# Three results written by VectorE behind the last maximum, later banks for output tiles and exponentials in pairs: an attention and feed-forward kernel on one core

## The chip, the cores and the metric

The kernel runs on one core of a Trainium2 chip. The metric is the device time of one execution in microseconds (us), as the median of several runs. The engines of the core are named as in the profile: PE (matrix products; PEld is its weight loading), DVE (VectorE), ACT (ScalarE), POOL (GpSimd) and SP (SyncE, which issues all DMAs here). SBUF is the on-chip memory; PSUM has eight banks of 512 fp32 columns, into which PE writes.

## The reference

The input x has 2048 rows of 512 values. It is normalized by row; an attention block with 32 heads of 16 values and a gated feed-forward block of width 1792 both take the normalized rows, and their results are added to x:

```python
xn = _layernorm(x, axis=-1)
q, k, v = (xn @ wqkv), split into 32 heads of 16
p = softmax(q @ k.T * 16 ** -0.5)          # 2048 x 2048 for each head
attention = (p @ v, heads side by side) @ wo
ffn = (silu(xn @ w1) * (xn @ w3)) @ w2
out = x + attention + ffn
```

## The kernel before, in words

**Tiling.** The query rows are cut into four blocks of 512 (`qc`), the 32 heads into eight groups of four (`g`). One block and group make a piece of work that is cut into units: two of 256 query rows, and for the last four groups four of 128 rows. In the last group of the last block the four units are called A, B, C and D here; D is the last unit of the kernel.

**What a unit goes through.**

- Maxima: PE computes scores with 128 query rows on the partitions (L1041, two banks at a time), and DVE takes the maximum of each row (L1081, 1024 columns at a time). From these come the negated maximum `negm` (L1217 on DVE for the last units, POOL otherwise) and two bf16 values of it, `Z` (L1165, L1167).
- Query tile: for the last four units `Z` is added to the query by a PE tile named `AQ` (`tile_QT2`), whose result ACT writes to `QT` (L810). Earlier units get it by DMA.
- Scores: PE computes them again, now with the keys on the partitions (L1303). One block of four matmuls of 128 columns fills one bank and is the input of one exponential. ACT takes the exponential of a bank (L1316, 512 columns) or of two neighbouring banks in one instruction (L1346, 1024 columns) and writes to a slot of `PT`.
- Value products: PE multiplies `PT` by the values (`tile_PV`, emitted at L566). For the last three units (B, C, D) it also sums the exponentials with a matrix of ones, DVE takes the reciprocal (L1402) and multiplies (L1404). For the units before, A among them, ACT copies the bank to `U` (L1412); then follow a DMA to `Lc` (L1433), a power on POOL (L1437), a DMA to memory (L1442), a DMA back to all partitions (`R`, L1446) and a product on POOL (L1457). The result is the normalized head `ON`.
- Output: rows of the first three blocks are finished by `tile_OUT`. For each 128 rows of the last block, `tile_OUTA` sums x, the feed-forward part and the first six head groups, and ACT writes the sum to one of four buffers (`t1`, `a32`, `th`, `zg`; L938). `tile_OUTB` multiplies the last two head groups by `wo`, DVE adds the buffer (L952), and SP issues the store (L907).

**What sets the order.** Nothing is ordered by the hardware here: a planner in Python (`_Prog` and the `pick_` functions) keeps a model of when each engine is free and when each operand is ready, picks in each step the operation that can start first, and writes the order out, with semaphore waits between engines. PE's candidates are the scores of L1041 (`p1_cand`), those of L1303 (`p2_cand`), the groups of matmuls of the active tiles (`col_cand`) and filling matmuls (`fill_cand`), whose results nobody reads.

**Banks.** Until the last maximum is issued, banks 0 to 3 belong to the maxima and banks 7, 6, 5, 4 to everything else; from then on (`red_n[0] >= NP1`) all eight are shared. A tile is a tenant of its bank from `give` until its result is written. `assign` hands out banks to tiles, `score_bank` chooses a bank for a score block, and `p2_cand` lets at most four blocks wait for their exponential. In the last stretch `assign` starts a new tile while fewer than five banks have tenants, and the `OUTB` tiles, in order, take a bank as soon as their `OUTA` is written; the tile then waits for its heads group by group (`g_on`). `exp_pair` makes one instruction of two blocks when their banks are neighbours and the second is ready within 0.02 us of the planner's model (`PAIR_WAIT`).

**Queues.** A tile's result goes to `miscq` (ACT) or to `redq` (DVE), which is served first in, first out; the items for `Z` of the last unit are put at its head.

**Filling.** `fill_cand` adds matmuls of the identity while a running count of PE columns (`low_load`) is under a bound.

Of the kernel before, what the change touches and what calls it, by code (L numbers as in the profile page):

```python
# [8 lines left out]
ALU = mybir.AluOpType  # L9
# [244 lines left out]
def _build(nc, A_x, A_wqkv, A_wo, B_w1, B_w3, B_w2, out):  # L254
# [19 lines left out]
    PAIR_DEPTH = 3  # L274
    PAIR_GAP = 1
    LAZY_GAP = 0.02
    MIN_PIECE = 1
    HI_LEAD = 0.0
    LAZY_MAX = 3.0
# [3 lines left out]
    MATE = 0.0  # L283
# [64 lines left out]
    with ctx:  # L348
# [449 lines left out]
        def tile_QT2(u):  # L798
            qc, g, q0, nq = units[u]
            qs = (qc * NG + g) % 3  # L800
            par = u % 2
            groups = qt_groups(qc, g, q0, nq, False)
            for qt in range(nq // 128):
                groups.append((lambda bk, qt=qt: col_groups(
                    bk, lambda i, z=32: Z[:, par, qt, 32 * i:32 * i + z], lambda i: ident[:, :], 128, c0=qt * 128,
                    start=False, stop=True, skip=True),
                    [("Z", par), ("ident",)], _c_mm(128), None))

            def evac(bk):
                return [_Item(lambda e: e.activation(QT[:, qs, q0:q0 + nq], bank(bk)[:, 0:nq], ACTF.Identity),  # L810
                              [("ps", bk)], qh_keys(qs, q0, nq), _c_act(nq), cb=lambda op: done.add(("AUG", u)))]
            return _Tile("AQ%d" % u, groups, evac, need=-1, cols=4 * nq)
# [97 lines left out]
        def tile_OUT(tg):  # L910
# [4 lines left out]
            def evac(bk):  # L915
                def cb(op):
                    store(tg)
                    done.add(("OUT", tg))
                    if tg + NXR < NT:
# [5 lines left out]
                         and all(("hT", qc * FC + fc) in done for fc in range(FC))  # L925
                         and all(("ON", qc, g, ts) in done for g in range(NG)), paced=True)

        def tile_OUTA(tg):
            qc, ts = divmod(tg, 4)
            groups = [g_x(tg)] + [g_h(tg, fc, NGA == 0 and fc == FC - 1) for fc in range(FC)]  # L930
            groups += [g_on(qc, ts, g, False, g == NGA - 1) for g in range(NGA)]

            def evac(bk):
                def cb(op):
                    done.add(("OUTA", tg))
                    if tg + NXR < NT:
                        load_xr(tg + NXR)
                return [_Item(lambda e: e.activation(opart[ts], bank(bk), ACTF.Identity),  # L938
                              [("ps", bk)], OP_KEYS[ts], _c_act(512), cb=cb)]
            return _Tile("OUTA%d" % tg, groups, evac, pred=lambda: ("xr", tg) in done  # L940
                         and all(("hT", qc * FC + fc) in done for fc in range(FC))
                         and all(("ON", qc, g, ts) in done for g in range(NGA)))

        def tile_OUTB(tg):
            qc, ts = divmod(tg, 4)
            groups = [g_on(qc, ts, g, g == NGA, g == NG - 1) for g in range(NGA, NG)]

            def evac(bk):
                def cb(op):
                    store(tg)  # L950
                    done.add(("OUT", tg))
                return [_Item(lambda e: e.tensor_tensor(osb[:, tg % 4, :], bank(bk), opart[ts], ALU.add),  # L952
                              [("ps", bk)] + OP_KEYS[ts], [("osb", tg % 4)], _c_dve(512), cb=cb)]
            return _Tile("OUTB%d" % tg, groups, evac, pred=lambda: ("OUTA", tg) in done and ("ST", tg - 4) in done)


        def split_rows(u):
# [292 lines left out]
        def score_bank(up=False):  # L1250
            mates = {it.exp[0] for it in expq[-1:]}
            best = (None, 0.0)
            for b in pool_banks():
                if b in bank_tenant or b in p2_busy:
                    continue
                r = P.ready("pe", (), [("ps", b)])
                if b - 1 in mates or (b + 1 in mates and not up):
                    r -= MATE
                if best[0] is None or r < best[1] - 1e-6:
                    best = (b, r)  # L1260
            return best

        def p2_cand():
# [2 lines left out]
                return None  # L1266
            n = p2_n[0]
            b, b_rd = score_bank()
            if b is None or len(p2_busy) >= 4:
                return None  # L1270
            qc, g, q0, nq = units[u]
            kpb = 512 // nq
# [82 lines left out]
        def tile_PV(u):  # L1355
# [37 lines left out]
            def evac(bk):  # L1393
# [15 lines left out]
                def cb(op):  # L1409
                    nrm_wait.append(u)  # L1410
                    nrm_next()
                return [_Item(lambda e: e.activation(U[:, us, 0:nq], bank(bk)[:, 0:nq], ACTF.Identity),  # L1412
                              [("ps", bk)], [("U", us)], _c_act(nq), cb=cb)]
            return _Tile("PV%d" % u, groups, evac, cols=4 * nq)
# [116 lines left out]
        def assign():  # L1531
# [17 lines left out]
            if crit and crit[0].name.startswith("AQ"):  # L1549
                bk = free_bank(TILE_BANKS if p2_n[0] and red_n[0] < NP1 else None)[0]  # L1550
                if bk is not None:
                    give(crit.pop(0), bk)
            if not head_tiles and sum(b in bank_tenant for b in pool_banks()) < (1 if red_n[0] < NP1 else 5):
                bk = free_bank(TILE_BANKS if red_n[0] < NP1 else None)[0]
                t = None if bk is None else choose()
                if t is not None:
# [15 lines left out]
        def col_cand():  # L1572
# [34 lines left out]
            def emit():  # L1607
# [8 lines left out]
                if not t.groups:  # L1616
# [8 lines left out]
                        if cb0 is not None:  # L1625
                            cb0(op)
                    last.cb = cb
                    if t.name.startswith("OUTB") or (t.name.startswith("PV") and int(t.name[2:]) in FAST_PV):
                        redq.extend(items)
                    else:  # L1630
                        miscq.extend(items)
# [141 lines left out]
        def pick_act():  # L1773
            a = cand("act", expq[0]) if expq else None
            pair, mate = None, 0
            for k in range(1, min(len(expq), PAIR_DEPTH)):
# [3 lines left out]
                if two is None:  # L1780
                    continue
                a2 = cand("act", two)
                if a2 <= a + PAIR_WAIT and (red_n[0] >= NP1 or sum(b_ in bank_tenant for b_ in pool_banks()) <= PAIR_TEN):
                    a, pair, mate = a2, two, k
                    break
            m = None
# [155 lines left out]
```

## Time and profile before

| what | before |
|---|---|
| time, median of 3 runs | 1196.95 us (1196.06 to 1197.04) |
| the profiled execution | 1196.41 us, of which the span from first to last instruction is 1194.7 us |
| busy: PE, DVE, ACT, POOL | 97%, 98%, 98%, 38% of the span |
| granted TensorE clock, mean | 0.999 |
| maxima on DVE (L1081) | 1018 instructions, 1217 ns each |
| single exponentials on ACT (L1316) | 1680 instructions, 628 ns each |
| paired exponentials on ACT (L1346) | 184 instructions, 1075 ns each |
| last maximum ends, last exponential ends | about 1170.5 us, 1189.2 us from the span's start |

A row of a timeline gives the start in us from the span's start, the time from there to the end of the last instruction of the group, the engine, the line, the operation, what it writes and reads with the shapes, the count, and in brackets the idle time before with what ended it. Neighbouring instructions of one engine overlap by a few hundredths to some tenths of a us, so lengths add up to more than the time that passes. Matmul records show the length of one pass through the array, which overlaps the next.

### The profile page before, as it was taken

The page shows a single profiled execution, that of the slowest core. Times are in us where ns is not written, and L with a number is a line of the kernel's source. Part 1 is how long each engine was busy: PE and PEld are TensorE (multiplying, and loading weights), DVE is VectorE, ACT ScalarE, POOL GpSimd, SP SyncE. Part 2 cuts the span into 40 slices and gives each one's busy share as a digit, 9 for nine tenths or more (in the row PEclk, how much of TensorE's full clock was granted, in tenths as well). Part 3 has the DMA queues.
Part 4 walks back from the last instruction along what each step waited for, and adds up shares of the span by engine and source line. Part 5 has one row for each costly group of instructions (what it writes and reads, how often), then busy time and mean ns, then how long its engine had stood idle before and what let it go on. Part 6 is the DMA issues. An engine that isn't in the chain of part 4 may idle for free.

```text
span 1194.7 us, 33930 instructions
## 1 busy us (share of the span) xinstructions
PE 1154.4 (97%) x14172; PEld 482.5 (40%) x14172; DVE 1172.0 (98%) x1067; ACT 1169.5 (98%) x2236; POOL 455.3 (38%) x912
## 2 busy tenths in 40 slices
PE   9999999999999999999999999999999999999998
PEld 4433333333334333333334434343333333345554
DVE  8999999999999999999999999999999999999994
ACT  7899999999999999999999999999999999999997
POOL 4453752433432255343422236634222215333320
PEclk9999999999999999999999999999999999999999
DMA  6523222111111021111100122211000111000000
GB/s 183 128 59 83 68 65 79 39 33 41 38 24 36 25 71 40 41 32 31 33 20 24 35 59 51 51 31 37 22 20 20 32 33 43 19 22 18 18 18 25
DMA packets 131189, 52.17 MB, mean 44 GB/s; under 512 B 100068, under 2 KB 131036, under 8 KB 131036
## 3 DMA queue, kind: packets, MB, share of 16 engines
q1 hardware_dynamic: 131036, 50.01, 16.9%
q8 instruction: 111, 1.82, 0.7%
q14 instruction: 42, 0.34, 0.1%
HBM read 38.73 MB, written 6.74 MB: 38 GB/s over the span
## 4 chain that ended last, share of the span: by engine, by line
PE 45%; ACT 44%; DVE 6%; issue 2%; DMA 2%; POOL 1%; ACTq 0%; POOLq 0%
ACT PT L1316 30%; PE ps L562 17%; PE ps L1303 13%; PE ps L566 8%; ACT PT L1346 7%; PE ps L1041 7%; DVE part L1081 6%; ACT zg L856 2%; ACT th L850 1%; ACT ub L860 1%; DMA R<-rd 1%; ACT U L1412 1%; ACT kq L750 1%; PE ps L1663 1%; DMA Lc<-U 0%
## 5 line engine op out<-in xcount | busy, mean ns | idle before, releaser
L1081 DVE TENSOR_REDUCE part<-ps 128x2 f32<-128x1024 f32 x1018 | 1153.0, 1217 | 1.9 <-PE ps L1041 1.7
L1316 ACT ACTIVATE PT<-ps 128x512 bf16<-128x512 f32 x1680 | 889.2, 628 | 5.6 <-PE ps L1303 2.5
L1303 PE MATMUL ps<-QT,KT 32*128 32x256 bf16 (+1 forms) x4672 | 544.5, 259 | 4.7 <-ACT PT L1346 3.7
L1041 PE MATMUL ps<-KT,QT 32*128 32x512 bf16 x2042 | 424.3, 384 | 2.4 <-DVE part L1081 2.3
L1303 PEld LDWEIGHTS ps<-QT,KT 32*128 32x128 bf16 x4672 | 207.4, 92 | 214.1 <-issue 110.7
L1437 POOL TENSOR_TENSOR Rc<-Lc,mone 128x8 f32<-128x8 f32 (+1 forms) x70 | 105.9, 1513 | 294.6 <-DMA Lc<-U 294.4
L1346 ACT ACTIVATE PT<-ps 128x1024 bf16<-128x1024 f32 x184 | 194.6, 1075 | 0.0
L562 PE MATMUL ps<-xnT,ident 128*128 128x512 bf16 (+3 forms) x646 | 177.4, 341 | 17.5 <-DVE part L1081 6.7
L566 PE MATMUL ps<-PT,Vaug 128*17 128x256 bf16 (+1 forms) x4672 | 179.6, 261 | 3.1 <-ACT PT L1316 1.3
L562 PE MATMUL ps<-xnT,w 128*128 128x512 bf16 (+3 forms) x637 | 153.2, 321 | 4.7 <-ACT ub L860 1.3
L1041 PEld LDWEIGHTS ps<-KT,QT 32*128 32x128 bf16 x2042 | 107.8, 91 | 122.5 <-DVE part L1081 56.8
L566 PEld LDWEIGHTS ps<-PT,Vaug 128*17 128x17 bf16 x4672 | 84.2, 89 | 89.1 <-issue 69.5
L562 PEld LDWEIGHTS ps<-xnT,ident 128*128 128x128 bf16 x646 | 47.4, 97 | 99.9 <-ACT PT L1316 44.5
L562 PEld LDWEIGHTS ps<-xnT,w 128*128 128x128 bf16 x637 | 44.9, 97 | 85.6 <-issue 52.9
L562 PE MATMUL ps<-w,hT 128*128 128x512 bf16 (+3 forms) x330 | 75.1, 315 | 0.0
L837 POOL TENSOR_TENSOR a<-zg,ub 128x512 f32<-128x512 bf16 x56 | 64.5, 1152 | 21.6 <-ACT ub L860 21.6
L839 POOL TENSOR_TENSOR hT<-a,t 128x512 bf16<-128x512 f32 x56 | 71.0, 1267 | 2.4
L1188 POOL TENSOR_TENSOR mx<-part 128x16 f32<-128x16 f32 (+1 forms) x67 | 14.1, 210 | 141.0 <-DVE part L1081 140.5
L1457 POOL TENSOR_TENSOR wk_on<-U,R 128x256 bf16<-128x256 f32 (+1 forms) x37 | 23.3, 630 | 85.8 <-DMA R<-rd 85.6
L835 POOL TENSOR_SCALAR t<-th 128x512 f32<-128x512 bf16 x56 | 34.7, 619 | 44.8 <-ACT th L850 43.2
L1457 POOL TENSOR_TENSOR on_b<-U,R 128x256 bf16<-128x256 f32 (+1 forms) x33 | 23.4, 709 | 70.9 <-DMA R<-rd 70.9
L850 ACT ACTIVATE th<-zg 128x512 bf16<-128x512 bf16 x56 | 37.7, 673 | 0.0
(104 smaller groups left out, 574.5 us busy)
## 6 DMA issues: line engine op xcount, KB each, us to landing
w<-in_B_w_dram SPq DMA_DIRECT2D x112, 128.0 KB
R<-rd SPq DMA_DIRECT2D x55, 128.0 KB
QT<-qd SPq DMA_DIRECT2D x31, 128.0 KB
KT<-kd SPq DMA_DIRECT2D x28, 128.0 KB
PT<-in_A_x_dram SPq DMA_DIRECT2D x4, 512.0 KB
xr<-in_A_x_dram SPq DMA_DIRECT2D x16, 128.0 KB
out_dram<-osb SPq DMA_DIRECT2D x16, 128.0 KB
qd<-kq SPq DMA_DIRECT2D x15, 128.0 KB
```

The costliest lines, as they stand in the source:

```text
L562: return e.matmul(bank(bk)[:, c0 + a:c0 + b], make_lhsT(0, 128), rhs_ap(0)[:, a:b], start=start, stop=stop, **kw)
L566: ins = e.matmul(bank(bk)[32 * i:32 * i + m, c0 + a:c0 + b], make_lhsT(i), rhs if (a, b) == (0, ncols) else rhs[:, a:b], start=start, stop ...
L837: q.append(_Item(lambda e: e.tensor_tensor(a32[:, :], zg[:, ss, :], ub[:, ss, :], ALU.mult), [("zg", ss), ("ub", ss)], [("a32",)], 1.1, 1.25))
L839: q.append(_Item(lambda e: e.tensor_tensor(hT[:, hslot(idx), :], a32[:, :], t1[:, :], ALU.mult), [("a32",), ("t1",)], [("hT", hslot(idx))] ...
L850: lazyq.append(_Item(lambda e: e.activation(th[:, ss, :], zg[:, ss, :], ACTF.Tanh), [("zg", ss)], [("th", ss)], 0.52, cb=part_done))
L1041: ins = e.matmul(bank(2 * sl + i), QT[32 * j:32 * j + 32, qs, q * 128:(q + 1) * 128], KT[32 * j:32 * j + 32, g, c_ * 512:(c_ + 1) * 512], ...
L1081: redq.append(_Item(lambda e: e.tensor_reduce(dst, pair_ap.rearrange("p (a b) -> p a b", b=512), AX.X, ALU.max), writes, [("part", par, qt ...
L1303: ins = e.matmul(bank(b)[:, i * nq:(i + 1) * nq], KT[32 * j:32 * j + 32, g, (k0 + i) * 128:(k0 + i + 1) * 128], QT[32 * j:32 * j + 32, qs, ...
L1316: expq.append(_Item(lambda e: e.activation(PT[:, sl, :], bank(b), ACTF.Exp, scale=SCALE), [("ps", b)], [("PT", sl)], _c_act(512), cb=cb, e ...
L1346: return _Item(lambda e: e.activation(PT[:, s0:s1 + 1:s1 - s0, :], ps8[:, b0:b1 + 1:b1 - b0, :], ACTF.Exp, scale=SCALE), [("ps", b0), ("ps ...
L1437: poolq["nrm"].append(_Item(lambda e: e.tensor_tensor(Rc[:, pp, 0:nl], Lc[:, pp, 0:nl], mone[:, 0:nl], ALU.pow), [("Lc", pp), ("mone",)], ...
L1457: poolq["nrm"].append(_Item(lambda e: e.tensor_tensor(onorm[ob][:, g, q0:q0 + nq], U[:, us, 0:nq], R[:, pp, 0:nq], ALU.mult), [("U", us)] ...
```

## The change

It concerns only decisions that the planner makes from the last maximum on; the constants that hold before that point stay as they were.

- `to_dve()` is true once the last score block for the maxima has been put on PE. A tile that finishes then has its result written by DVE with a `tensor_scalar` (times 1, plus 0) instead of by ACT: an `AQ` tile (`QT`), an `OUTA` tile (one of the four buffers), a `PV` tile of a unit without the fast path (`U`). Such an item is named `dve` and goes to `redq`.
- An `OUTB` tile gets a bank only when its last two head groups are finished; the last of them (`OUTB_EARLY`) when all but the last group is.
- A new tile is started while fewer than two banks have tenants (`TAIL_TEN`), not five.
- A bank beside the one of the last waiting score block is preferred even if it is ready up to 0.3 us later (`TAIL_MATE`); before, by 0.0.
- Two blocks are paired if the second is ready within 0.05 us (`TAIL_WAIT`), not 0.02.
- `TAIL_BUSY` is 4, the number that was written there before.

```diff
+    OUTB_EARLY = 1
+    TAIL_BUSY = 4
+    TAIL_TEN = 2
+    TAIL_MATE = 0.3
+    TAIL_WAIT = 0.05
+    TAIL_DVE = 1
...
+        def to_dve():
+            return TAIL_DVE and p1_n[0] >= NP1
+
...
             def evac(bk):
+                if to_dve():
+                    return [_Item(lambda e: e.tensor_scalar(QT[:, qs, q0:q0 + nq], bank(bk)[:, 0:nq], 1.0, 0.0,
+                                                            ALU.mult, ALU.add),
+                                  [("ps", bk)], qh_keys(qs, q0, nq), _c_dve(nq), cb=lambda op: done.add(("AUG", u)),
+                                  name="dve")]
                 return [_Item(lambda e: e.activation(QT[:, qs, q0:q0 + nq], bank(bk)[:, 0:nq], ACTF.Identity),
                               [("ps", bk)], qh_keys(qs, q0, nq), _c_act(nq), cb=lambda op: done.add(("AUG", u)))]
...
+                if to_dve():
+                    return [_Item(lambda e: e.tensor_scalar(opart[ts], bank(bk), 1.0, 0.0, ALU.mult, ALU.add),
+                                  [("ps", bk)], OP_KEYS[ts], _c_dve(512), cb=cb, name="dve")]
                 return [_Item(lambda e: e.activation(opart[ts], bank(bk), ACTF.Identity),
                               [("ps", bk)], OP_KEYS[ts], _c_act(512), cb=cb)]
...
-            return _Tile("OUTB%d" % tg, groups, evac, pred=lambda: ("OUTA", tg) in done and ("ST", tg - 4) in done)
+            return _Tile("OUTB%d" % tg, groups, evac, pred=lambda: ("OUTA", tg) in done and ("ST", tg - 4) in done
+                         and all(("ON", qc, g, ts) in done for g in range(NGA, NG if tg < NT - OUTB_EARLY else NG - 1)))
...
                 if b - 1 in mates or (b + 1 in mates and not up):
-                    r -= MATE
+                    r -= MATE if red_n[0] < NP1 else TAIL_MATE
...
-            if b is None or len(p2_busy) >= 4:
+            if b is None or len(p2_busy) >= (4 if red_n[0] < NP1 else TAIL_BUSY):
                 return None
...
+                if to_dve():
+                    return [_Item(lambda e: e.tensor_scalar(U[:, us, 0:nq], bank(bk)[:, 0:nq], 1.0, 0.0,
+                                                            ALU.mult, ALU.add),
+                                  [("ps", bk)], [("U", us)], _c_dve(nq), cb=cb, name="dve")]
                 return [_Item(lambda e: e.activation(U[:, us, 0:nq], bank(bk)[:, 0:nq], ACTF.Identity),
                               [("ps", bk)], [("U", us)], _c_act(nq), cb=cb)]
...
-            if not head_tiles and sum(b in bank_tenant for b in pool_banks()) < (1 if red_n[0] < NP1 else 5):
+            if not head_tiles and sum(b in bank_tenant for b in pool_banks()) < (1 if red_n[0] < NP1 else TAIL_TEN):
...
-                    if t.name.startswith("OUTB") or (t.name.startswith("PV") and int(t.name[2:]) in FAST_PV):
+                    if items[0].name == "dve" or t.name.startswith("OUTB") or (t.name.startswith("PV") and int(t.name[2:]) in FAST_PV):
                         redq.extend(items)
...
-                if a2 <= a + PAIR_WAIT and (red_n[0] >= NP1 or sum(b_ in bank_tenant for b_ in pool_banks()) <= PAIR_TEN):
+                if a2 <= a + (PAIR_WAIT if red_n[0] < NP1 else TAIL_WAIT) and (red_n[0] >= NP1 or sum(b_ in bank_tenant for b_ in pool_banks()) <= PAIR_TEN):
```

The order that the planner writes out for the changed kernel is the same as before on all engines until the last maximum. Behind it the three `tensor_scalar` writes stand on DVE directly after the two `Z` writes (`zg`, then `U`, then `QT`), and ACT's last stretch reads, with x for a count of single exponentials and P for a pair:

```
before: x11 zg x1 U x1 P QT x9 P x2 P x16
after:  x12 P x2 P x1 P x5 P x1 P x1 P x1 P P x1 P x1 P x1
```

## The prediction

> **What bounds the kernel now.** I read the page's totals first, then the order of instructions built from both kernels, then the timelines of the last 31 us, engine by engine, and last the chain of waits there.
>
> ```profile
> span 1194.7 us, 33930 instructions
> PE 1154.4 (97%) x14172; PEld 482.5 (40%) x14172; DVE 1172.0 (98%) x1067; ACT 1169.5 (98%) x2236; POOL 455.3 (38%) x912
> ```
>
> Three engines are full over the whole span, so totals decide nothing. The built order does: all five engines have the same order in both kernels up to the last score maximum; PE first differs just behind the block of 4 scores at 1169.11, ACT at the twelfth exponential of its last stretch, DVE behind the two Z writes. So only the tail counts, from about 1169.5 us to the end. It lasts 25 us; ACT carries it, and its timeline is:
>
> ```profile
> 1164.11 5.58 ACT L1316 ACTIVATE PT<-ps 128x512 bf16<-128x512 f32 x11
> 1169.57 0.61 ACT L938 ACTIVATE zg<-ps 128x512 f32<-128x512 f32 x1
> 1170.05 0.62 ACT L1316 ACTIVATE PT<-ps 128x512 bf16<-128x512 f32 x1
> 1170.61 0.28 ACT L1412 ACTIVATE U<-ps 128x128 f32<-128x128 f32 x1
> 1170.99 0.60 ACT L1316 ACTIVATE PT<-ps 128x512 bf16<-128x512 f32 x1
> 1171.48 1.02 ACT L1346 ACTIVATE PT<-ps 128x1024 bf16<-128x1024 f32 x1
> 1172.38 0.28 ACT L810 ACTIVATE QT<-ps 128x128 bf16<-128x128 f32 x1
> 1173.08 1.57 ACT L1316 ACTIVATE PT<-ps 128x512 bf16<-128x512 f32 x3 [0.41 <-PE ps L1303]
> 1175.28 3.04 ACT L1316 ACTIVATE PT<-ps 128x512 bf16<-128x512 f32 x6 [0.63 <-PE ps L1303]
> 1178.21 1.03 ACT L1346 ACTIVATE PT<-ps 128x1024 bf16<-128x1024 f32 x1
> 1179.13 1.23 ACT L1316 ACTIVATE PT<-ps 128x512 bf16<-128x512 f32 x2
> 1180.26 1.02 ACT L1346 ACTIVATE PT<-ps 128x1024 bf16<-128x1024 f32 x1
> 1181.16 8.05 ACT L1316 ACTIVATE PT<-ps 128x512 bf16<-128x512 f32 x16
> ```
>
> Columns: start, length, engine, line, what, count, idle before. Neighbours overlap, so I count by pitch, from one start to the next. The last row: 8.05 less one length of 0.62, over 15 steps, is 0.495 for a single exponential. A pair takes 0.90 (1171.48 to 1172.38), 0.92 (1178.21 to 1179.13) and 0.90 (1180.26 to 1181.16); I use 0.91. The last exponential ends at 1189.21.
>
> Ledger from 1169.57 to 1189.09, where a next instruction could start: 29 singles 14.36, 3 pairs 2.73, the zg write 0.48 (to 1170.05), U and QT about 0.16 each (1152.53 to 1152.68 is such a step elsewhere), in all 17.89 of 19.52. So **1.63 us are gaps**. Behind 1175.28, where 24 singles and 2 pairs make 13.70 of 13.81, only 0.11. The gaps sit between 1170 and 1175.3, where PE is late.
>
> ```profile
> 1152.53 0.27 ACT L1412 ACTIVATE U<-ps 128x128 f32<-128x128 f32 x1
> 1152.68 2.56 ACT L1316 ACTIVATE PT<-ps 128x512 bf16<-128x512 f32 x5
> ```
>
> ```profile
> 1169.11 0.39 PE L1303 MATMUL ps<-QT,KT 32*128 32x128 bf16 x4
> 1169.43 1.13 PE L566 MATMUL ps<-PT,Vaug 128*17 128x128 bf16 x68
> 1170.56 0.78 PE L1303 MATMUL ps<-QT,KT 32*128 32x128 bf16 x12
> ...
> 1171.82 0.40 PE L562 MATMUL ps<-xnT,wq_last 128*128 128x128 bf16 x4
> ...
> 1173.53 0.23 PE L566 MATMUL ps<-PT,Vaug 128*17 128x128 bf16 x4
> ...
> 1174.53 0.39 PE L562 MATMUL ps<-wo,wk_on 128*128 128x512 bf16 x1
> 1174.85 0.42 PE L1303 MATMUL ps<-QT,KT 32*128 32x128 bf16 x12
> 1175.20 1.18 PE L562 MATMUL ps<-wo,wk_on 128*128 128x512 bf16 x4
> ...
> 1189.27 0.23 PE L566 MATMUL ps<-PT,Vaug 128*17 128x128 bf16 x4 [0.89 <-ACT PT L1316]
> ...
> 1191.28 0.40 PE L562 MATMUL ps<-wo,wk_on 128*128 128x512 bf16 x1 [1.39 <-DVE wk_on L1404]
> ```
>
> PE runs 72 value products from 1169.43 without a score between them; the next 12 scores (three exponentials) start at 1170.56. Behind ACT's last exponential stands a fixed end: products at 1189.27, then
>
> ```profile
> 1162.48 8.02 DVE L1081 TENSOR_REDUCE part<-ps 128x2 f32<-128x1024 f32 x7
> ...
> 1170.95 0.18 DVE L1167 TENSOR_TENSOR Z<-negm,Z 128x4 bf16<-128x4 f32 x1
> 1174.65 0.96 DVE L1402 RECIPROCAL R<-ps 128x128 f32<-128x128 f32 x1 [3.53 <-PE ps L566]
> 1175.64 0.29 DVE L1404 TENSOR_TENSOR wk_on<-ps,R 128x128 bf16<-128x128 f32 x1
> ...
> 1189.94 0.96 DVE L1402 RECIPROCAL R<-ps 128x128 f32<-128x128 f32 x1 [4.86 <-PE ps L566]
> ...
> 1191.72 0.69 DVE L952 TENSOR_TENSOR osb<-ps,zg 128x512 bf16<-128x512 f32 x1 [0.49 <-PE ps L562]
> ```
>
> the reciprocal, the last output product and the last sum to 1192.41, and 2.29 us for the store. From the end of the last exponential to the span's end that is 5.49 us. The changed order ends with the same instructions, so the time follows the end of ACT's last exponential. DVE, between 1171.13 and 1174.65, stands idle: room for three moved writes.
>
> **The change part by part.**
>
> **Three writes to VectorE.** The zg write (last OUTA tile), U (unit A) and QT (unit D) leave ACT: 0.48 + 0.16 + 0.16 = 0.80 us less there. In the built order they stand on DVE directly behind the Z writes, so they start at 1171.16. The trace has no such DVE copy out of PSUM. Its bounds for 512 columns are 0.40 (a scaling from SBUF) and 0.69 (the output sum at 1191.72); I take 0.69, which also reads PSUM, and for 128 columns the 0.29 of the product at 1175.64, with 0.16 (ACT's step) as the other end. Between these ends the three end at most 0.5 earlier, which moves nothing that ACT waits for.
>
> ```profile
> L629 DVE TENSOR_SCALAR osb<-PT,mv,lnr 128x512 bf16<-128x512 bf16 x6 | 2.1, 399 | 0.0
> ```
>
> So zg ends at 1171.85, U at 1172.2, QT at 1172.5, all before the reciprocal behind them is due (1174.8). Their new waiters are PE's third batch of scores, which takes the banks of zg and U, and the fourth, which takes that of QT. PE reaches them at about 1172.18 and 1173.53; the third batch loses at most 0.1. U is 1.3 later than on ACT (1170.89), and with it a chain through SP's queue and POOL:
>
> ```profile
> 1170.91 0.53 SPq L1433 DMA_DIRECT2D Lc<-U  x1
> 1179.04 0.45 POOL L1457 TENSOR_TENSOR wk_on<-U,R 128x128 bf16<-128x128 f32 x1 [5.26 <-DMA R<-rd]
> ```
>
> That chain ended at 1179.49 and will end near 1180.8. Behind its DMAs on SP stand only the four stores, none due before 1182.4. Its head is read by an output product that PE reaches at about 1180.7; behind it on PE stands the ninth batch of scores.
>
> **More pairs.** The built order has the same 46 exponentials in ACT's last stretch, but 26 singles and 10 pairs where there were 40 and 3. Seven more pairs at 2 x 0.495 - 0.91 = 0.08 save 0.56 us.
>
> [...] The pitches show 0.08, since neighbours overlap; the sum goes by them.
>
> **Banks only when ready, two tile tenants instead of five.** Output tiles no longer hold banks while they wait, so scores get them. In the built order PE breaks the 72 products after 12 for a batch of 12 scores. Walked with the rows' costs (12 scores 0.35 from 1174.85 to 1175.20; 8 pairs of products 1.00 from 1173.53 to 1174.53; 4 output products 1.18, the row at 1175.20; the AQ tile about 0.4), and with each instruction's semaphore waits, PE starts the batches at 1169.71, 1170.90, 1172.18, 1173.53, 1175.31, 1176.98, 1178.32, 1179.61, 1181.2, 1182.6, 1183.4, 1184.8; scores can be read 0.45 later. ACT, without gaps, wants them at 1170.06, 1171.5, 1172.9, 1174.3, 1175.8, 1177.7, 1179.1, 1180.5, 1181.9, 1183.3, 1184.2, 1185.6. The first comes 0.1 late, the fifth is a tie, the others are 0.15 to 0.45 early. So most of the 1.63 us of gaps goes. I keep 0.3: 0.1 for the first, as much as the 0.11 behind 1175.28, and 0.1 for the fifth.
>
> **Sum.** From 1169.57, 15 singles 7.43 and 10 pairs 9.10 make 16.53 (before: 19.52), which is 2.99 less: 0.80 for the writes, 0.56 for pairs, 1.63 for gaps. With 0.3 of gaps left the gain is **2.7 us**. The profiled execution took 1196.41 (span 1194.7 and 1.7 around it), so 1193.7 (span 1192.0). The median of the runs shown, 1196.95, lies 0.54 above that execution; from it, **1194.2**.
>
> **The rivals.** *PE stays late* (a wait in place of the one removed). For it: all PE's margins are under 0.6, and the head of unit A, through two DMAs, arrives just when PE wants it. The same hop elsewhere takes 0.82 more:
>
> ```profile
> 67.43 2.65 DMA R<-rd
> ...
> 73.20 3.47 DMA R<-rd
> ```
>
> With that the ninth batch starts near 1182.0 instead of 1181.2 and ACT waits 0.5: gain 2.2, time 1194.8. If all 1.63 us of gaps come back elsewhere the gain is 1.36: 1195.6. Against it: behind 1175.28, with a much tighter PE, gaps were 0.11. *The changed order isn't run as written, no gain*: 1196.9; excluded almost wholly by the built order.
>
> *Slower: PE's clock falls.* The planner puts 9 filling passes of 512 columns behind the last maximum instead of some 14. If the clock halved from the fifth batch on, PE's last 10 us (1175.3 to 1185.4) take 20, products end near 1195.4 instead of 1189.9, span 1200.2, time 1202.4. It decides once over 3 us of PE's work runs at half rate, as that eats the gain.
>
> ```profile
> 1170.50:1175.00 4.50, 4.35 (x168) 3.28 (x161) 0.87 (x5) 3.64 (x8) 1.01 (x1) 1.00 0.06 8
> 1185.00:1189.20 4.20, 3.37 (x115) 2.17 (x113) 0.08 (x1) 4.20 (x9) 0.00 (x0) 1.00 0.11 35
> ```
>
> Against it: with PE busy 3.37 of 4.20 (second figure, then the other engines; the clock is the 1.00) the clock stayed full. My longest PE wait before the last products is about 0.5, less than the 0.89 there. How long a wait it takes no row here shows. [...]
>
> **How the numbers follow.** A measurement of this kernel tells about 0.2%, 2.4 us, from no change, so 1194.6 is the border. The forecast (gain 2.4 to 3.0) has 0.62; a late PE (gain 0.5 to 2.4) 0.31; no gain 0.02; the clock 0.05. Hence faster 0.62, same 0.33, slower 0.05. The range starts at no gap at all, 1194.0, less the 0.8 by which the lowest run lay under its median: 1193.2. It ends at 1195.7, with all gaps back.
>
> **What would show it.** Right: ten pairs; the last exponential ending near 1186.5; three DVE copies between 1171.1 and 1172.6; 5.5 us from the last exponential to the end; ACT's idle time behind 1169.6 under 0.5. Wrong: ACT waiting for L1303's scores over 1 us in all, PE standing before the output product for POOL's head, DVE copies over 0.7, or a clock under 1.00 before 1186.

## The result and the profile after

| | before | after |
|---|---|---|
| time, median (lowest to highest), 13 runs each | 1196.95 us (1195.88 to 1201.46) | 1194.47 us (1193.72 to 1195.57) |
| ratio, 95% interval | | 0.9976 [0.9968, 0.9984] |
| span of the profiled execution | 1194.7 us | 1193.3 us |
| last maximum ends; last exponential ends | 1170.50; 1189.21 | 1170.93; 1187.81 |
| tail: last maximum to the span's end | 24.19 us | 22.34 us |
| last exponential to the span's end | 5.48 us | 5.47 us |

The change is faster by 2.48 us in the medians. A second batch of the same kernel on another chip gave 1194.61 us, ratio 0.9981 [0.9972, 0.9991], and a tail of 22.12 us. The two spans differ by only 1.4 us because the last maximum ends 0.43 later in this profile, with the same code up to it (in the second batch's profile it ends at 1170.36). So I compare tails: 1.85 and 2.07 us shorter. The medians differ by some half a microsecond more; that is less than half the width of the ratio's interval (about 1 us), and I don't explain it. Each tail is read from one profiled execution, and the two of this same kernel differ by 0.22, so smaller differences of tails say nothing.

The page's totals still tell nothing:

```profile
span 1193.3 us, 33766 instructions
PE 1125.6 (94%) x14015; PEld 480.5 (40%) x14172; DVE 1172.8 (98%) x1070; ACT 1168.3 (98%) x2226; POOL 455.5 (38%) x912
```

PE's 157 missing matmuls are missing records: its weight loads are 14172 as before.

ACT's timeline, columns as in the prediction:

```profile
1164.54 6.07 ACT L1334 ACTIVATE PT<-ps 128x512 bf16<-128x512 f32 x12
1170.63 1.02 ACT L1364 ACTIVATE PT<-ps 128x1024 bf16<-128x1024 f32 x1
1171.55 1.08 ACT L1334 ACTIVATE PT<-ps 128x512 bf16<-128x512 f32 x2
1172.51 1.04 ACT L1364 ACTIVATE PT<-ps 128x1024 bf16<-128x1024 f32 x1
1173.41 0.63 ACT L1334 ACTIVATE PT<-ps 128x512 bf16<-128x512 f32 x1
1173.88 1.07 ACT L1364 ACTIVATE PT<-ps 128x1024 bf16<-128x1024 f32 x1
1174.79 2.80 ACT L1334 ACTIVATE PT<-ps 128x512 bf16<-128x512 f32 x5
1177.47 1.03 ACT L1364 ACTIVATE PT<-ps 128x1024 bf16<-128x1024 f32 x1
1179.02 0.60 ACT L1334 ACTIVATE PT<-ps 128x512 bf16<-128x512 f32 x1 [0.52 <-PE ps L1321]
...
1187.19 0.62 ACT L1334 ACTIVATE PT<-ps 128x512 bf16<-128x512 f32 x1
```

No write of zg, U or QT is left, pairs stand where singles stood, and in the whole stretch one wait is left, at 1179.02, for scores. The pair at 1177.47 would have let the next one start at 1178.38 (pitch 0.91), so 0.64 us are lost there; the five singles from 1174.79 take 2.68 instead of 2.48, 0.20 lost. By the prediction's ledger, 17.68 us from 0.93 ahead of the last maximum's end to where an instruction could start behind the last exponential (0.125 ahead of its end), less 16.53 of work, gaps are **1.15 us**, not 0.3; in the second batch 0.92; before, 1.63. (Counting late steps alone, without the early ones that net out, gives 1.33 and 1.04.)

DVE has taken the three writes:

```profile
1171.46 0.69 DVE L953 TENSOR_SCALAR zg<-ps 128x512 f32<-128x512 f32 x1
1172.07 0.28 DVE L1431 TENSOR_SCALAR U<-ps 128x128 f32<-128x128 f32 x1
1172.26 0.28 DVE L817 TENSOR_SCALAR QT<-ps 128x128 bf16<-128x128 f32 x1
1175.54 0.96 DVE L1420 RECIPROCAL R<-ps 128x128 f32<-128x128 f32 x1 [3.00 <-PE ps L572]
...
1190.31 0.69 DVE L969 TENSOR_TENSOR osb<-ps,zg 128x512 bf16<-128x512 f32 x1 [0.48 <-remote]
```

0.69, 0.28 and 0.28 us, in DVE's idle time, which ends at 1175.54. PE's timeline shows where ACT's wait comes from:

```profile
1174.30 0.42 PE L1321 MATMUL ps<-QT,KT 32*128 32x128 bf16 x12
1174.64 0.23 PE L572 MATMUL ps<-PT,Vaug 128*17 128x128 bf16 x4
1174.70 0.23 PE L572 MATMUL ps<-PT,ones_t 128*32 128x128 bf16 x4
...
1176.07 0.43 PE L1321 MATMUL ps<-QT,KT 32*128 32x128 bf16 x16
1176.43 0.23 PE L572 MATMUL ps<-PT,Vaug 128*17 128x128 bf16 x4
1176.49 0.23 PE L572 MATMUL ps<-PT,ones_t 128*32 128x128 bf16 x3
1177.43 0.23 PE L572 MATMUL ps<-PT,ones_t 128*32 128x128 bf16 x1 [0.71 <-issue]
...
1178.59 0.42 PE L1321 MATMUL ps<-QT,KT 32*128 32x128 bf16 x12
...
1181.18 0.23 PE L572 MATMUL ps<-PT,Vaug 128*17 128x128 bf16 x2 [0.35 <-issue]
```

At 1176.49 PE issues three of a group of four matmuls with ones and starts the fourth 0.94 us later, at 1177.43. The next scores, which ACT waits for, start at 1178.59. "issue" is time in which PE waited for nothing that the profile shows: no semaphore is named for it. The chain of waits takes the same way (start, length, what):

```profile
1176.50 0.22 PE ps L572 x7
1176.72 0.71 issue
1177.43 1.23 PE ps L572 x57
1178.66 0.34 PE ps L1321 x12
```

**What PE stands for.** PE's instructions come by DMA. In the tail the queue list of the trace (queue: packets, MB, share) has, for 1169 to 1190:

```profile
q8 instruction: 5, 0.08, 1.7%
```

0.08 MB in five packets is 16 KB each. The page counts 111 of them for 28344 instructions of PE (matmuls and weight loads), so a packet holds 256: 128 matmuls with their 128 weight loads. The stops fit this. Numbered by weight loads, PE stands ahead of matmul 13701, 13829 and 13957, 128 apart; I call these places borders. The trace has the packets that came last before the three restarts starting at 1171.06, 1174.82 and 1178.58; PE goes on at 1173.68, 1177.43 and 1181.17, 2.60 to 2.63 later each time, having stood 0.34, 0.98 and 0.57 (from one weight load to the next; the idle time in brackets of a row is shorter, as it starts at the end of the matmul before). The last two packets start 1.15 after PE has passed the border before (1173.68 to 1174.82, 1177.43 to 1178.58). 1.15 and 2.60 make **3.75 us** from one stop's end to the next one's. Where PE enters a block without having stood, its packet starts sooner: 0.56 behind the border at matmul 13573 (1170.50 to 1171.06), so that the next border was passed 3.18 later, stop included. The four-matmul groups at 1174.64 and 1174.70 are 0.056 apart; at that rate PE is through a block in 1.8 us. In the profile of before PE stood 0.41 at the first of these borders (1173.20); the packet of the next started at 1174.35, again 1.15 later, but PE came to that border only at 1178.67, since its order had the larger tiles ahead of it:

```profile
1173.21 0.39 PE L1303 MATMUL ps<-QT,KT 32*128 32x128 bf16 x4
...
1178.02 0.61 PE L562 MATMUL ps<-xnT,ident 128*128 128x512 bf16 x2
...
1178.67 0.23 PE L566 MATMUL ps<-PT,Vaug 128*17 128x128 bf16 x4
```

### The profile page after: what moved, and what is told of

The parts are those of the page before. It is cut to its first block, busy times and chain, and to the rows that moved or that the text cites. A ratio compares the mean times of both kernels' runs of the same rounds, so it can differ in the third digit from the quotient of the medians.

```text
span 1193.3 us, 33766 instructions
## 1 busy us (share of the span) xinstructions
PE 1125.6 (94%) x14015; PEld 480.5 (40%) x14172; DVE 1172.8 (98%) x1070; ACT 1168.3 (98%) x2226; POOL 455.5 (38%) x912
## 4 chain that ended last, share of the span: by engine, by line
ACT 51%; PE 40%; DVE 6%; issue 3%; POOL 0%; DMA 0%; SPq 0%; ACTq 0%; another core or an unknown queue 0%; POOLq 0%
ACT PT L1334 35%; PE ps L568 14%; PE ps L1321 12%; ACT PT L1364 8%; PE ps L572 7%; PE ps L1059 6%; DVE part L1099 6%; ACT zg L867 2%; ACT th L861 1%; ACT ub L871 1%; ACT U L1434 1%; ACT kq L756 1%; PE ps L1685 1%; ACT xnT L677 0%; ACT Vaug L771 0%
## 5 line engine op out<-in xcount | busy, mean ns | idle before, releaser
L1364 ACT ACTIVATE PT<-ps 128x1024 bf16<-128x1024 f32 x191 | 201.9, 1073 | 0.0
L568 PE MATMUL ps<-xnT,ident 128*128 128x512 bf16 (+3 forms) x572 | 157.7, 335 | 25.7 <-DVE part L1099 6.3
L568 PE MATMUL ps<-xnT,w 128*128 128x512 bf16 (+3 forms) x597 | 143.9, 316 | 9.9 <-ACT U L1434 4.4
L568 PE MATMUL ps<-w,hT 128*128 128x512 bf16 (+3 forms) x312 | 72.1, 311 | 3.3 <-ACT U L1434 2.1
L1479 POOL TENSOR_TENSOR wk_on<-U,R 128x256 bf16<-128x256 f32 (+1 forms) x37 | 23.3, 631 | 87.7 <-DMA R<-rd 87.6
```

The costliest lines, as they stand in the source:

```text
L568: return e.matmul(bank(bk)[:, c0 + a:c0 + b], make_lhsT(0, 128), rhs_ap(0)[:, a:b], start=start, stop=stop, **kw)
L1364: return _Item(lambda e: e.activation(PT[:, s0:s1 + 1:s1 - s0, :], ps8[:, b0:b1 + 1:b1 - b0, :], ACTF.Exp, scale=SCALE), [("ps", b0), ("ps ...
L1479: poolq["nrm"].append(_Item(lambda e: e.tensor_tensor(onorm[ob][:, g, q0:q0 + nq], U[:, us, 0:nq], R[:, pp, 0:nq], ALU.mult), [("U", us)] ...
```

## The experiments

**Theory (supply):** the remaining gaps come from the blocks of PE's instructions, a floor of 3.75 us for each 128 matmuls of the tail (the runs below narrow this: 3.5 to 4.0 from one stop to the next, less where PE has not stood before). **Rivals:** the stops belong to the work at that place (a wait that the profile doesn't name); or the tail is ACT's ledger alone, and the stops cost nothing. "Tail" and "gaps" (ledger) are as above. In the profiles of no_dve (span 1198.5) and nfpv2_fill_one (1195.3) PE's granted clock is 0.50 for 10.2 us from 1148.3 and for 6.8 us from 1146.8, where all kernels have the same code; just before, PE waits 1.11 and 0.88 us there for a DMA. These two profiles are read from the last maximum on only.

| kernel | time, median | ratio to before [95%] | tail | gaps | pairs/singles |
|---|---|---|---|---|---|
| again (unchanged) | 1194.61 | 0.9981 [0.9972, 0.9991] | 22.12 | 0.92 | 10/15 |
| ones_halves | 1200.17 | 1.0030 [1.0013, 1.0047] | 27.47 | 5.02 | 10/15 |
| fill_one | 1194.11 | 0.9976 [0.9967, 0.9985] | 21.81 | 0.61 | 10/15 |
| shift46 | 1197.41 | 1.0004 [0.9995, 1.0014] | 22.68 | 1.01 | 10/15 |
| dve_only | 1196.25 | 0.9994 [0.9985, 1.0004] | 24.30 | 2.43 | 4/27 |
| no_dve | 1195.11 | 0.9989 [0.9976, 1.0002] | 22.70 | 0.71 | 10/15 |
| no_pairs | 1195.60 | 0.9989 [0.9980, 0.9999] | 22.91 | 1.49 | 7/21 |
| no_banks | 1196.34 | 0.9995 [0.9986, 1.0004] | 23.65 | 2.46 | 10/15 |
| no_fill | 1194.39 | 0.9986 [0.9976, 0.9995] | 22.17 | 0.91 | 9/17 |
| nfpv2 | 1193.73 | 0.9982 [0.9973, 0.9991] | 21.69 | 0.47 | 9/17 |
| nfpv2_nofill | 1195.53 | 0.9989 [0.9979, 0.9998] | 21.46 | 0.16 | 8/19 |
| nfpv2_fill_one | 1194.41 | 0.9983 [0.9974, 0.9992] | 21.98 | 0.53 | 9/17 |

Rows one to four ran on one chip, the next four on another, the next three on a third; the medians of before there were 1196.49, 1196.70 and 1196.16, and 1196.42 for the last row.

### The same kernel again

No edit.

> The changed kernel once more. In its first profile the tail (end of the last maximum to the end of the span) took 22.4 us, and PE stood still three times at a place with no semaphore wait, in front of its matmuls 13701, 13829 and 13957 (counted from 0 over the whole program), 128 apart, each time until 2.6 us after a 16 KB packet of the DMA queue q8 (instruction) began. Theory A, PE's instructions come in blocks of 128 matmuls (256 instructions with the weight loads) and the tail uses them up faster than they are fetched: the same three places again, within one matmul, each ending 2.5 to 2.7 us after a packet's start; tail 22.1 to 22.6. Theory B, the stops were stray ones of one execution: other places or none, tail 21.4 to 21.8, as the prediction's walk had it.

PE stands ahead of the same three matmuls by number; the last two:

```profile
1176.63 0.23 PE L572 MATMUL ps<-PT,ones_t 128*32 128x128 bf16 x1 [0.43 <-issue]
...
1180.37 0.23 PE L572 MATMUL ps<-PT,Vaug 128*17 128x128 bf16 x2 [0.35 <-issue]
```

The packets ahead of these started at 1174.31 and 1177.78, so the restarts are 2.32 and 2.59 behind them, the first sooner than the 2.5 to 2.7 that was expected. From the first restart (1173.16) to the second it takes 3.47 here, to the third 3.74. The stops repeat; their length varies by some tenths of a us.

### More instructions for the same products

The matmuls with ones of the fast units are cut into two of half the columns: 192 more instruction pairs, the same number of columns.

```diff
...
-                    f2 = col_groups(bk, lambda j: ones_t[:, 0:32],
-                                    lambda j: PT[:, sls[j], i0 * nq:(i0 + 1) * nq], nq, c0=256,
+                    f2 = [col_groups(bk, lambda j: ones_t[:, 0:32],
+                                     lambda j, h=h: PT[:, sls[j], i0 * nq + h * hq:i0 * nq + (h + 1) * hq], hq,
+                                     c0=256 + h * hq, start=False, stop=kt == NT - 1, skip=True, own=True)
+                          for h in range(2)]
...
```

> The same order on every engine, but each of the 192 matmuls that sum the exponentials for units B, C and D is cut into two of 64 columns, so PE gets 192 matmuls more and the same columns. Theory A (instruction supply, 3.76 us for 128 matmuls): up to 192 / 128 x 3.76 = 5.6 us longer, 4 to 5.6 with what slack there is; time about 1199. Theory B (array time and semaphores set PE's pace): columns are the same, at most 1 us longer; time 1194.4 to 1195.5.

Tail 27.47, 5.1 to 5.4 over the two profiles of the changed kernel; the median 5.56 over that of the first row. 192 matmuls are 1.5 blocks, and 1.5 x 3.75 is 5.6. PE:

```profile
1177.22 0.23 PE L572 MATMUL ps<-PT,ones_t 128*32 128x64 bf16 x5 [2.24 <-issue]
...
1180.97 0.24 PE L572 MATMUL ps<-PT,ones_t 128*32 128x64 bf16 x1 [0.23 <-issue]
...
1184.71 0.24 PE L572 MATMUL ps<-PT,ones_t 128*32 128x64 bf16 x6 [0.70 <-issue]
```

The restarts are 3.75 and 3.74 us apart, at matmuls 13829, 13957 and 14085; the restart ahead of them, 1173.20, is 4.02 earlier. ACT waits behind the first:

```profile
1179.35 1.08 ACT L1334 ACTIVATE PT<-ps 128x512 bf16<-128x512 f32 x2 [3.32 <-PE ps L1321]
```

Another border falls into the last products: PE stands 1.02 there, and the end behind the last exponential grows from 5.48 to 6.73. The supply sets the time here; a ledger of columns or of ACT's work would have left it unchanged.

This is also the only run in which the clock falls between the last maximum and the last exponential: behind the longest stop it is 0.50 from about 1177.8 to 1181.2. In the windows view (length, busy time of PE, PEld, DVE, ACT, POOL, then PE's clock, DMA share, GB/s):

```profile
1174.35:1177.77 3.42, 1.18 (x86) 0.91 (x84) 0.02 (x1) 1.68 (x4) 0.42 (x1) 1.00 0.04 5
1177.77:1181.18 3.41, 3.18 (x115) 1.99 (x111) 1.23 (x2) 1.83 (x3) 0.46 (x1) 0.50 0.08 24
```

It doesn't set the time, as PE still reaches the next border before its block is there and stands 0.23.

### Fewer instructions for the same filling

From the last maximum on, the four-tile filling pass becomes one matmul of the full array: 18 matmuls less.

```diff
-                                 own=P.pe_mode == "col" and not P.pe_full),
+                                 own=P.pe_mode == "col" and not P.pe_full,
+                                 n=1 if red_n[0] >= NP1 and P.pe_mode == "col" and not P.pe_full else 4),
```

> The same order, but a filling pass behind the last maximum that was four matmuls of 32 output rows is one of them: 18 matmuls fewer, with the same array time of each pass. Theory A: up to 18 / 128 x 3.76 = 0.5 us shorter, and the stops stand 18 or fewer matmuls later in the work. Theory B: the same time within 0.1, and no stop moves.

18 of 128 of 3.75 us is 0.53. The tail is shorter by 0.53 and 0.31 than the two of the changed kernel, the median by 0.50 than that of the first row, though the intervals of the two ratios overlap. The largest stop is left, its idle time between the 0.71 and 0.43 of the changed kernel's two profiles:

```profile
1176.55 0.23 PE L572 MATMUL ps<-PT,Vaug 128*17 128x128 bf16 x4 [0.61 <-issue]
```

### The borders moved

46 warm-up matmuls at the start of the kernel are cut in two, so each block border falls 46 matmuls earlier in the work of the tail.

```diff
-                    P.pe(lambda e: e.matmul(bank(bk)[:, 0:256], ones_t[:, :],
-                                            ones_t[:, :].unsqueeze(1).broadcast_to([128, 2, 128]),
-                                            start=True, stop=True),
+                    def two(e):
+                        e.matmul(bank(bk)[:, 0:128], ones_t[:, :], ones_t[:, :], start=True, stop=True)
+                        return e.matmul(bank(bk)[:, 128:256], ones_t[:, :], ones_t[:, :], start=True, stop=True)
+                    P.pe(two,
...
```

> The same order, but each of 46 warm-up matmuls of 256 columns at the start is cut into two of 128 columns; nothing of the tail is touched. Theory A: the borders of the blocks of 128 move by 46 matmuls, so the stops come again at counts 5 above a multiple of 128, which is 46 matmuls earlier in the work; tail within 0.7 us of 22.4 either way. Theory B: nothing in the tail moves; tail 21.4 to 22.4.

```profile
1178.93 0.23 PE L572 MATMUL ps<-PT,Vaug 128*17 128x128 bf16 x3 [0.82 <-issue]
...
1188.29 0.24 PE L572 MATMUL ps<-PT,ones_t 128*32 128x128 bf16 x4 [0.30 <-issue]
```

The stop at 1178.93 is ahead of matmul 13957, as in the changed kernel, but at another piece of work; a border now falls into the last products (1188.29), and the end behind the last exponential is 5.94 instead of 5.48. At the three places in the work where the changed kernel stood 0.34, 0.98 and 0.57 the weight loads are 0.003 apart here. So the stops go by number, not by work. The restart at 1188.29 is 3.16 behind its packet's start, more than elsewhere; a store of the output moves at the same time, and the packet took 1.78 instead of the 1.18 to 1.32 of those ahead of the stops in after. The median is 2.8 us over the first row's, far more than the tail's 0.3 to 0.6; the profiled execution, 1195.05, was the quickest of runs from 1195.05 to 1199.19, so what the others lost isn't seen, and stays open.

### One part of the change at a time

The three DVE writes alone, with the old bank and pair rules:

```diff
-    TAIL_TEN = 2
-    TAIL_MATE = 0.3
-    TAIL_WAIT = 0.05
+    TAIL_TEN = 5
+    TAIL_MATE = 0.0
+    TAIL_WAIT = 0.02
...
-            return _Tile("OUTB%d" % tg, groups, evac, pred=lambda: ("OUTA", tg) in done and ("ST", tg - 4) in done
-                         and all(("ON", qc, g, ts) in done for g in range(NGA, NG if tg < NT - OUTB_EARLY else NG - 1)))
+            return _Tile("OUTB%d" % tg, groups, evac, pred=lambda: ("OUTA", tg) in done and ("ST", tg - 4) in done)
```

> Of the change only the three writes by VectorE; banks, tenants and pair limits as before (4 pairs in ACT's last stretch instead of 10; 635 matmuls behind the last score product for a maximum, as before and after). Tail = from the end of the last maximum to the end of the span: 24.2 before, 22.1 to 22.3 after. Ledger theory (the end follows ACT's work and PE only has to be early, as the prediction had it): ACT loses 0.8 of work and one pair's 0.08, gaps stay: tail 23.3. Supply theory (PE's blocks of 128 matmuls set the pace): as many matmuls as before, so it helps only where ACT and not PE was late: 23.3 to 24.2.

The tail is 24.30, no shorter than before: 0.80 us left ACT and came back as gaps (2.43 instead of 1.63). ACT, then PE of this kernel:

```profile
1170.40 1.08 ACT L1333 ACTIVATE PT<-ps 128x512 bf16<-128x512 f32 x2 [0.53 <-PE ps L1320]
1172.01 0.60 ACT L1333 ACTIVATE PT<-ps 128x512 bf16<-128x512 f32 x1 [0.52 <-PE ps L1320]
```

```profile
1169.97 0.68 PE L1320 MATMUL ps<-QT,KT 32*128 32x128 bf16 x8
...
1171.58 0.85 PE L1320 MATMUL ps<-QT,KT 32*128 32x128 bf16 x12
```

Both waits are for scores behind PE's long row of value products, which this order doesn't break. The writes had filled time in which ACT would have waited. A third wait, 0.42 at 1182.53, follows a stop of 0.38 at matmul 13957. Of the tail, 0.2 lies behind ACT: the last output product takes 0.61 instead of 0.40, at a clock of 0.50, and the end is 5.68 instead of 5.48. The ledger theory's 23.3 is missed by 1.0, the supply theory's range by 0.1.

The other way round, the change without the three writes (`TAIL_DVE = 0`):

```diff
-    TAIL_DVE = 1
+    TAIL_DVE = 0
```

> The change without the three writes by VectorE: they stay on ACT (639 matmuls in the tail instead of 634). Ledger theory: ACT has 0.8 more to do, tail 22.9 to 23.1. Supply theory: ACT stood still for 1.3 us in the tail of the changed kernel, waiting for PE, and this takes up most of the 0.8: tail 22.2 to 22.6.

Tail 22.70, 0.4 to 0.6 longer than with them: of the 0.80 on ACT about a half to three quarters count, as the gaps fall to 0.71. This lies between the two theories' ranges.

Without the wider limits for pairs:

```diff
-    TAIL_MATE = 0.3
-    TAIL_WAIT = 0.05
+    TAIL_MATE = 0.0
+    TAIL_WAIT = 0.02
```

> The change with the old pair limits: no bank preferred, 0.02 us of patience; 7 pairs instead of 10 in ACT's last stretch, 646 matmuls in the tail instead of 634 (12 more of the fill). Ledger theory: three pairs at 0.08 are lost, tail 22.4 to 22.5. Supply theory: 12 matmuls more at 0.029 us, 0.35: tail 22.4 to 22.7. The two differ little here; a change of more than 0.5 would speak against both.

Tail 22.91, 0.6 to 0.8 longer, with three pairs fewer, which are worth 0.24. By what was expected, more than 0.5 speaks against both theories. The rest fits supply but isn't separated from the new order: the planner put 12 more matmuls into this tail, and ACT's longest wait comes 1.7 us after a stop at matmul 13957 (restart at 1179.80):

```profile
1181.49 1.02 ACT L1364 ACTIVATE PT<-ps 128x1024 bf16<-128x1024 f32 x1 [0.72 <-PE ps L1321]
```

Without the two bank rules (`TAIL_TEN = 5` and the old condition of `OUTB`, as above):

```diff
-    TAIL_TEN = 2
+    TAIL_TEN = 5
```

> The change without its bank rules: up to five tenants, output tiles take a bank before their heads are ready; writes by VectorE and pair limits stay (10 pairs; 613 matmuls in the tail instead of 634, as 21 of the fill are gone). Ledger theory: PE is late with scores again, most of the 1.6 us of gaps of the kernel before come back: tail 23.2 to 23.8. Supply theory: 21 matmuls fewer at 0.029 us are 0.6 less: tail 21.6 to 22.2, unless waits for banks hold PE elsewhere.

Tail 23.65, 1.3 to 1.5 longer. Here the supply theory alone was wrong and the ledger right: PE stands at none of the borders (its first wait in the tail, at 1187.78, is for ACT), and ACT waits where dve_only does, behind the long row of products:

```profile
1171.15 1.08 ACT L1333 ACTIVATE PT<-ps 128x512 bf16<-128x512 f32 x2 [0.53 <-PE ps L1320]
1172.76 0.60 ACT L1333 ACTIVATE PT<-ps 128x512 bf16<-128x512 f32 x1 [0.52 <-PE ps L1320]
```

So the bank rules carry the change: they bring the scores forward, and without them the freed 0.80 us and the seven more pairs, together 1.36, shorten the tail by 0.54 only. The parts don't add.

### Taking instructions out

Three kernels thin PE's tail: no filling after the last maximum (no_fill), unit B on the path by `U` and POOL as unit A, without its matmuls with ones (nfpv2), and both (nfpv2_nofill).

```diff
-            if pv_u[0] >= NU or not low_load(P.free["pe"]):
+            if pv_u[0] >= NU or red_n[0] >= NP1 or not low_load(P.free["pe"]):
...
-    NFPV = 3
+    NFPV = 2
```

> The changed kernel without any filling matmul behind the last maximum (607 matmuls there instead of 634); this also tries the prediction's slower rival, that PE's clock falls with less filling. Supply theory: 27 matmuls fewer at 0.029 us, up to 0.8 less, so the tail is 21.4 to 21.8 instead of 22.1 to 22.3, and the clock stays full. Rival, the fill keeps the clock up: matmuls of the tail at twice their length somewhere behind 1175, tail 24 or more.

Tail 22.17 with 27 matmuls fewer: a miss. PE comes sooner to the second border and stands the longer:

```profile
1176.15 0.23 PE L572 MATMUL ps<-PT,Vaug 128*17 128x128 bf16 x4 [1.01 <-issue]
```

What was taken out was time in which the next block could come; the order of the rest also changed (nine pairs). In the windows view the clock stays full though PE is busy only 2.83 of 5.00:

```profile
1175.00:1180.00 5.00, 2.83 (x147) 2.06 (x139) 0.37 (x3) 4.39 (x7) 0.46 (x1) 1.00 0.08 17
```

> The changed kernel with unit B on the slow path (its exponentials are summed by the column of ones in the values, then DMAs and POOL, as for unit A), so that 64 matmuls with the matrix of ones go; the planner adds 9 filling ones: 579 instead of 634 in the tail. Supply theory: up to 1.6 us less, but ACT's work is the floor, with no gaps 21.1; so tail 21.2 to 21.7. Rival, PE is held by waits on ACT and not by supply: 22.0 to 22.4; or unit B's chain of some 8 us ends late and holds an output product: over 22.4.

55 matmuls fewer, no stop at the two borders where the changed kernel had its 0.98 and 0.57, tail 21.69, gaps 0.47.

> Both: unit B on the slow path and no filling matmul behind the last maximum, 543 matmuls in the tail instead of 634. Supply theory: supply could be 2.7 us shorter, so it binds no more and ACT is the floor: tail 21.0 to 21.4, no stop of over 0.1 us in front of a block's border. Rival, the clock falls or unit B's chain is late: 22 or more.

Tail 21.46, just over the range, gaps 0.16, and ACT's timeline shows no wait in brackets. This is what the prediction had counted on with its 0.3. The time doesn't follow: the profiled execution took 1193.26, but the median is 1195.53, with a mean clock of 0.996 to 0.999 in the executions. Where the clock fell in the longer ones no profile shows.

Last, nfpv2 with the single filling matmul:

```diff
-    NFPV = 3
+    NFPV = 2
...
+                                 n=1 if red_n[0] >= NP1 and P.pe_mode == "col" and not P.pe_full else 4),
```

> The version that the runs point to: unit B on the slow path, and a filling pass of four 32-row matmuls behind the last maximum made of one; filling stays, so that PE is as busy as in the run with unit B alone on the slow path (561 matmuls in the tail instead of 579 there). Supply theory: the last late scores (0.7 us of gaps on ACT in that run) go in part, tail 21.3 to 21.6 instead of 21.7, time 1193.3 to 1193.7, and no time over 1195 as without filling. Rival, the rest of the gaps come from semaphore waits: tail 21.6 to 21.8 and the same time.

Tail 21.98, median 1194.41, two of eleven times over 1195: a miss on each count, and nothing beyond nfpv2. Of the 0.29 by which the tail is longer than that of nfpv2, 0.23 lies behind the last exponential (5.66 instead of 5.43), where a border now falls into the last products and PE stands 0.33. The quickest kernel is nfpv2, 1193.73 us; its ratio to before, 0.9982 [0.9973, 0.9991], doesn't tell it from the changed kernel's 0.9976 [0.9968, 0.9984] on another chip, and only its tail, shorter by 0.4 to 0.65, speaks for it.

## Why the prediction was right, and where it was wrong

- **Time and sign.** 1194.2 forecast, 1194.47 measured, inside the range; faster by 0.24% by the ratio. The mechanism (ACT carries the tail, PE's scores set its gaps) is what the runs show. Two of its signs failed: the last exponential ended at 1187.81, 0.9 later than the 1186.5 moved by the 0.43 of the last maximum, and ACT's gaps were over 0.5, in the first profile even over the 1 us that it had named as a sign of being wrong. (The lowest of the three runs lay 0.89 under their median, not 0.8; the range would start at 1193.1.)
- **Three writes on DVE.** Forecast 0.69, 0.29 and 0.29 from 1171.16; measured 0.69, 0.28 and 0.28 from 1171.46, the last maximum being 0.43 later. The 0.80 off ACT is right as a term of this sum, but not by itself: alone it gives nothing, and left out it costs 0.4 to 0.6.
- **Pairs.** Ten, as built; from 1170.63 to 1171.55 and from 1172.51 to 1173.41 a pair takes 0.92 and 0.90, against 0.91; with 0.495 for a single these pitches save 0.07 and 0.09, against 0.08.
- **Fixed end.** 5.47 against 5.49.
- **POOL's head.** Forecast near 1180.8. It was there at 1180.50, ahead of the output product that reads it:

```profile
1180.05 0.45 POOL L1479 TENSOR_TENSOR wk_on<-U,R 128x128 bf16<-128x128 f32 x1 [4.82 <-DMA R<-rd]
```

```profile
1182.19 0.82 PE L568 MATMUL ps<-wo,wk_on 128*128 128x512 bf16 x3
```

  The rival that PE stays late came true in its effect and not by its price: PE was late, but not for this head.
- **The step that failed: "most of the 1.63 us of gaps goes. I keep 0.3".** The term measured 1.15, and 0.92 in the second profile; the excess of 0.85 and 0.62 is all by which the tails' gain falls short of 2.7. It came from the walk of PE's batches, which had only durations and semaphores. Moved by the 0.43 of the last maximum, the walk puts the first three batches at 1170.14, 1171.33 and 1172.61, where they were (1170.14, 1171.33, 1172.64). The fourth was due at 1173.96 and started at 1174.30, the sixth at 1177.41 and 1178.59, the eighth at 1180.04 and 1181.50: 0.34, 1.18 and 1.46 late. These steps of 0.34, 0.84 and 0.28 follow the three borders, where PE stood 0.34, 0.98 and 0.57; the last two steps are smaller than their stops, so PE made part of them up. In ACT's margins of 0.15 to 0.45 the first about fits, the second doesn't. The fifth batch, named as a tie, cost 0.20.
- **Why no row of before showed it.** There the packets of the first two borders started 3.78 apart, as in the changed kernel (3.76), but PE reached the second border 4.3 us after its packet started, 1.7 more than the 2.6 of the changed kernel's stops. The bank rules bring the products together, and so make the stop; without them (no_banks) there is none. The 0.41 at the first border was in the trace of before, and the prediction didn't use it.
- **The slower rival.** No fall of the clock before the last exponential: 1.00 in the windows of after from 1170.93 to 1188, and in no_fill, where PE stood up to 1.16. How long a wait it takes the prediction left open, and these runs give no single length: behind the 2.24 us of ones_halves the clock was 0.50, behind the waits of 1.11 and 0.88 in no_dve and nfpv2_fill_one too, and behind the 1.16 of no_fill it was 1.00.
- **Luck.** By the profiled tails the gain is 1.85 to 2.07, 0.6 to 0.85 under the forecast 2.7; the medians show 2.48. That the forecast time was met to 0.3 is partly the spread of single executions.

## What to carry to other kernels

When an order is made denser, walk the engine that feeds the bottleneck also by its count of instructions: here, behind a stop, the next 256 of PE's came 3.5 to 4.0 us after the 256 before, while small matmuls with their weight loads would use them in 1.8 (groups of four 0.056 apart in after). A stop that falls between equal matmuls, is named "issue", and comes back every 128 matmuls was such a border here; cutting matmuls in two moved it (46 matmuls earlier in the work in shift46) or made more of them (ones_halves, tail 27.47), and fewer, larger ones went with a tail shorter by 0.31 to 0.53 (fill_one), though in no_fill, with 27 matmuls fewer, the tail stayed at 22.17 and the stop grew from 0.98 to 1.16. Work taken off the bottleneck was worth something only where its operands came earlier too (dve_only, with 0.80 us off ACT: tail 24.30 against 24.19): test the parts apart before adding their prices.

## What was not expected of the hardware

The stops at blocks of instructions. By the traces the packets are 16 KB, five of them 0.08 MB, and the stops stand 128 matmuls apart, 256 instructions with the weight loads. In the tail of the changed kernel a packet starts once PE has entered the block before it, 0.56 to 1.7 us after. What was not expected is that PE stands for it: 0.34, 0.98 and 0.57 us in the changed kernel and up to 2.49 in ones_halves. In the tails of before and after PE goes on 2.60 to 2.63 us after the packet's start, in again 2.32 and 2.59, and later beside a store (2.86 in dve_only, 3.16 in shift46). So PE stood where it was through a block sooner than this and the packet's delay together, and didn't where it took longer: in before a block passed in 3.10 us without a stop (1178.68 to 1181.78), as its packet had started 0.21 after the entry. Over the whole kernel PE takes about 10.8 for a block (1193.3 us for 111 blocks), far more.
